# Attention and expert layers on one core: the lesser of two key tiles' negated scores is taken ahead of the exponentials, and the small constant of the softmax is added on ScalarE

## The chip, the cores and the metric

The kernel runs on one core of a Trainium2 chip, as one program. The metric is the device time of one execution in microseconds (us). The kernel before took 918.2 us (median of three runs, 917.75 to 921.53). Profiles are of one execution each.

Names used below: PE is TensorE's matmul pipe, PEld its weight load, DVE is VectorE, ACT is ScalarE, POOL is GpSimd, SP is SyncE, which issues the DMAs. SBUF is the on-chip memory, PSUM the banks that matmuls write.

## The reference, cut to what matters

Sliding-window attention (batch 4, 8 heads, 576 positions, head width 64, window 128) is followed by four experts whose outputs are mixed with given probabilities.

```python
scores = scale * np.matmul(q, k.transpose(0, 1, 3, 2))        # scale = 1/8
mask = (rel >= 0) & (rel < 128)                               # rel = query position - key position
scores = np.where(mask, scores + bias[None], -1000000000.0)   # bias = -slope * |rel|
scores = scores - np.max(scores, axis=-1, keepdims=True)
attn = np.exp(scores)
attn = attn / (np.sum(attn, axis=-1, keepdims=True) + 1e-09)
x = np.matmul(attn, v)                                        # then reshaped to 2304 tokens x 512
for e in range(4):
    h = np.maximum(x @ w1[e], 0.0)                            # 512 -> 1024
    out += p[:, e:e + 1] * (h @ w2[e])                        # 1024 -> 512
```

## The kernel before, in words

Products with float32 accuracy are made of two parts, a rounded high part and the low rest: each operand is cast to the high part (`cast`, L306, on ACT or DVE), the low part is operand minus high part (`minus`, L319, on DVE or POOL), and three matmuls (high by high, high by low, low by high) replace one. That is most of what DVE, ACT and POOL do for the experts' weights (tiles w1h, w1l, w2h, w2l) and for q, k and v (qs, kh, kl, vs).

The 2304 tokens are cut into seven blocks (`BLOCKS`, L195: three of 256, four of 384). A piece of weights is run over one or several blocks at a time. Attention for a later block is made while PE multiplies the experts of an earlier one. From about 506 us on there is no attention left and the experts of the last four blocks run in a form with seven block products instead of eight (`sevenfold`, L949).

Attention goes by units (`unit`, L487): one tile of 128 queries, two heads. A query tile sees its own 128 keys and up to 128 keys of the tile in front of it. Because the window is as wide as a tile, at each column of the two key tiles set on top of each other exactly one of the two keys is inside the window: the key in the earlier tile for columns right of the diagonal, the own one for the rest. The steps of a unit are, with their lines: scores on PE (L513); on DVE, for each head, bias added to the scores, negated and scaled, with the least value kept as the row's softmax maximum (L544, tile s of 256 columns a head, and tile t); on ACT the exponentials of each head with their sum (L556); on DVE 1e-9 added to the two sums (L571, two columns) and the reciprocal taken (L580); then the weights are multiplied by it (DVE L601 or ACT L609), transposed on PE (L627), split into high and low (L313, L323), cut into the two sides of the diagonal on POOL (L651), and multiplied with v (L698).

From block 2 on, a unit with an earlier tile is folded (`fold`, L587): the weights of the two key tiles are added to one tile of 128 columns (L592, on DVE or POOL) before they are multiplied, so that only one tile is transposed and split; L651 takes the sides apart again. There are 52 such units; 12 others (the 8 of block 1 and 4 of a tile that sees its own keys alone) are not folded, and the 8 of block 0 (`g.plain`) take a shorter way.

The order of all work is set by a planner (`Plan`, L42) in the kernel's own program: every operation is entered with the engines that it can run on, an assumed duration for each, a due time and what it reads and writes. The planner goes through time, gives each engine the operation that is due first among those that could start soon, and chooses the engine where there are two. An entry may also name a `port`: operations of DVE and POOL that name it are not planned to run at the same time (default: POOL's only). Each engine then runs its list in order, waiting on semaphores. A change of any cost or engine thus re-orders the lists of all engines, and shifts splits between DVE and POOL and casts between ACT and DVE.

Of the kernel before, what the change touches and what calls it, by code (L numbers as in the profile page):

```python
# [11 lines left out]
AF = mybir.ActivationFunctionType  # L12
ALU = mybir.AluOpType
# [3 lines left out]
NEG = -1.0e30  # L17
PE, DVE, ACT, POOL, SP = "PE", "DVE", "ACT", "POOL", "SP"
# [169 lines left out]
dve = lambda n: 0.065 + n / 960  # L188
dve2 = lambda n: 0.065 + n / 1920
pool = lambda n: 0.1 + n * 0.00256  # L190
# [12 lines left out]
FOLD = 2  # L203
# [25 lines left out]
def attention_moe(  # L229
# [13 lines left out]
    nc = tc.nc  # L243
    P = 128
# [12 lines left out]
    plan = Plan()  # L257
# [38 lines left out]
    bias = sb.tile([P, H, 2 * P], F32, tag="bias", name="bias")  # L296
# [4 lines left out]
    by = {DVE: nc.vector, POOL: nc.gpsimd}  # L301
# [38 lines left out]
    for us, nbs in passes:  # L340
        for u in us:
# [3 lines left out]
            if max(nbs) <= PAIRED and u % 2 == 0 and u + 1 in us:  # L345
                half_of[l], half_of[l + 1] = 0, 1
                for nb in nbs:
                    n = BLOCKS[nb][1]
# [14 lines left out]
            for nb in nbs:  # L363
                n = BLOCKS[nb][1]
# [25 lines left out]
    for nb, (s0, n) in enumerate(BLOCKS):  # L390
        for hp in range(NPAIR):
            g = Rec()
# [94 lines left out]
    def unit(u):  # L487
        g, pk, d = u.seg, u.pk, u.due
        n = pk + P

        o = P - pk
        edge = S - u.tile * P % S
        edge = edge if edge < P else 0
        bk, s, t = Buf("b"), Buf("acc" if g.plain else "s"), Buf("t")
        sv = lambda: s[:, : 4 * P].rearrange("p (h n) -> p h n", h=2) if s.tag == "acc" else s.place
        both = [(s, 0), (s, 1)]
# [27 lines left out]

        bkey = [("bias", g.hp)] if pk else [("bias", g.hp, 1)]
        bv = lambda: bias[:, hs, :]
        if edge:
# [7 lines left out]
            )  # L537
            bv, bkey = b2, [bb]
        if 0 < pk < P:
            plan.op({POOL: 0.3, DVE: 0.28}, lambda e: by[e].memset(sv()[:, :, :o], 0.0), d, ["scores"], both, port=())  # L540


        def least(h):
            return lambda e: nc.vector.tensor_tensor_reduce(  # L544
                out=sv()[:, h, o:],
                in0=sc()[:, h, :n],
                in1=bv()[:, h, o:],
                scale=-0.125,
                scalar=-NEG,
                op0=ALU.add,  # L550
                op1=ALU.min,
                accum_out=t[:, h : h + 1],
            )

        def exponents(h):
            return lambda e: nc.scalar.activation(  # L556
                sv()[:, h, o:],
                sv()[:, h, o:],
                AF.Exp,
                bias=t[:, h : h + 1],  # L560
                scale=-1.0,
                accum_out=t[:, 2 + h : 3 + h],
            )

        for h in range(2):
            plan.op({DVE: 0.15 + n / 960}, least(h), d + 0.3, [*bkey, bk], [(s, h), (t, h)])
        for h in range(2):
            plan.op({ACT: 0.29 + n * 0.00087}, exponents(h), d + 0.4, [(t, h)], [(s, h), (t, 2 + h)])
        plan.op(
            {DVE: 0.19},  # L570
            lambda e: nc.vector.tensor_scalar(  # L571
                out=t[:, 2:4], in0=t[:, 2:4], scalar1=1.0e-9, scalar2=None, op0=ALU.add
            ),
            d + 0.5,
            [],
            [(t, 2), (t, 3)],
# [5 lines left out]
            [(t, 2), (t, 3)],  # L582
            [(t, 4)],
        )


        fold = pk > 0 and g.nb >= FOLD  # L587
        o2, n2 = (P, P) if fold else (o, n)
        if fold:
            plan.op(  # L590
                {DVE: dve(2 * P), POOL: pool(2 * P)},
                lambda e: by[e].tensor_tensor(out=sv()[:, :, P:], in0=sv()[:, :, P:], in1=sv()[:, :, :P], op=ALU.add),  # L592
                d + 0.5,
                [(t, 2), (t, 3)],
                both,
                port=(DVE, POOL),
            )

        def weights_(e):
            if e == DVE:  # L600
# [557 lines left out]
    for hp in range(NPAIR):  # L1158
        hs = slice(2 * hp, 2 * hp + 2)
        for i, due in ((1, -37), (0, -33)):  # L1160
# [24 lines left out]
            out=dps, in0=dps, scalar1=1.0e-9, scalar2=None, op0=ALU.add  # L1185
# [9 lines left out]
            out=prob, in0=dp, in1=dps[:, :, None].to_broadcast([P, NT // P, E]), op=ALU.mult  # L1195
# [5 lines left out]
    for g in gs:  # L1201
        segment(g)
        for u in g.units:
            unit(u)
        gathered(g)
# [88 lines left out]
```

## Time and profile before

| | |
|---|---|
| runs | 917.75, 918.2, 921.53 us |
| profiled execution | 917.55 us, of which the span from first to last instruction is 915.8 us |
| PE busy | 890.8 us (97% of the span), at the full granted clock (0.999) |
| DVE busy | 735.0 us (80%), 1520 instructions |
| ACT busy | 454.3 us (50%) |
| POOL busy | 378.4 us (41%) |
| DMA | 105 GB/s mean |

Times are in us unless marked ns. A PE that is busy all the time is not losing time to waits; where its busy time falls short of a stretch, it waited, and the wait rows name what for. A mean duration of a group also holds what an instruction stood still inside.

### The profile page before, as it was taken

What the parts mean: (1) busy time and instruction counts of PE and PEld (TensorE: products, weight loads), DVE (VectorE), ACT (ScalarE), POOL (GpSimd) and SP (SyncE); (2) the same over time, 40 slices, a digit from 0 to 9 for tenths busy, and PEclk for the clock granted to TensorE, in tenths of its full rate; (3) what the DMA queues carried; (4) which work ended last, traced back from release to release, by engine and by line L of the source; (5) the groups of instructions that cost most, each with busy time, mean ns of one, the idle gap of its engine ahead of it and who ended that gap; (6) DMA issues with size and microseconds to landing.
All of it is one profiled execution on the core that took longest, in us unless ns stands there. A gap on an engine that the chain in (4) does not pass through costs nothing.

```text
span 915.8 us, 14430 instructions
## 1 busy us (share of the span) xinstructions
PE 890.8 (97%) x5108; PEld 805.5 (88%) x5108; DVE 735.0 (80%) x1520; ACT 454.3 (50%) x1089; POOL 378.4 (41%) x361
## 2 busy tenths in 40 slices
PE   7898999999999999989999999999999999999998
PEld 5787999999999998878899998989898998999897
DVE  4999887697888899989997997767876767677665
ACT  4976555364655466656664343435333433434341
POOL 2446545244444355577674663212632222222100
PEclk9999999999999999999999999999999999999999
DMA  9764534242444445443211022221232121212101
GB/s 241 234 213 160 176 123 137 81 136 67 136 135 135 131 155 178 157 127 98 82 49 67 24 90 72 68 70 52 87 116 92 47 93 47 89 50 76 40 1 70
DMA packets 39961, 96.20 MB, mean 105 GB/s; under 512 B 3792, under 2 KB 17488, under 8 KB 39888
## 3 DMA queue, kind: packets, MB, share of 16 engines
q1 hardware_dynamic: 39888, 95.28, 32.6%
q8 instruction: 40, 0.66, 0.3%
q14 instruction: 33, 0.27, 0.1%
HBM read 90.54 MB, written 4.72 MB: 104 GB/s over the span
## 4 chain that ended last, share of the span: by engine, by line
PE 84%; DVE 12%; ACT 2%; issue 1%; DMA 1%; ACTq 0%; DVEq 0%
PE b L1095 39%; PE b L907 18%; PE b L985 18%; PE av L698 3%; PE b L513 2%; PE b L627 2%; DVE w2l L323 1%; DVE s L544 1%; DVE s L592 1%; DVE w1l L323 1%; DMA k<-in_qk 1%; DVE acc L1113 1%; PE b L504 1%; DVE s L601 1%; DVE t L571 1%
## 5 line engine op out<-in xcount | busy, mean ns | idle before, releaser
L1113 DVE SCALAR_TENSOR_TENSOR acc<-b,prob,acc 128x512 f32<-128x512 f32 (+1 forms) x229 | 169.8, 743 | 66.5 <-PE b L1095 65.5
L1095 PE MATMUL b<-w2h,rh 128*128 128x512 f32 x440 | 174.1, 396 | 1.0 <-DVE rl L935 1.0
L1095 PE MATMUL b<-w2l,rh 128*128 128x512 f32 x440 | 172.9, 393 | 0.0
L1095 PE MATMUL b<-w2h,rl 128*128 128x512 f32 x440 | 172.5, 392 | 0.0
L907 PE MATMUL b<-xh,w1h 128*128 128x256 f32 (+1 forms) x528 | 160.9, 305 | 5.0 <-DVE t L544 2.1
L907 PE MATMUL b<-xl,w1h 128*128 128x256 f32 (+1 forms) x528 | 156.9, 297 | 0.5 <-DVE xl L323 0.5
L907 PE MATMUL b<-xh,w1l 128*128 128x256 f32 (+1 forms) x528 | 157.1, 297 | 0.0
L323 POOL TENSOR_TENSOR w2l<-w2r,w2h 128x512 fp32r<-128x512 f32 x45 | 67.7, 1507 | 124.9 <-ACT w2h L311 111.6
L907 PEld LDWEIGHTS b<-xh,w1h 128*128 128x128 f32 x528 | 100.2, 190 | 8.0 <-DVE t L544 2.3
L651 POOL TENSOR_SCALAR_AFFINE_SELECT pt<-s 128x512 fp32r<-128x512 f32 x104 | 66.9, 667 | 92.1 <-DVE s L323 68.5
L907 PEld LDWEIGHTS b<-xl,w1h 128*128 128x128 f32 x528 | 100.2, 190 | 2.9 <-DVE xl L323 0.7
L907 PEld LDWEIGHTS b<-xh,w1l 128*128 128x128 f32 x528 | 100.0, 189 | 0.0
L1095 PEld LDWEIGHTS b<-w2h,rl 128*128 128x128 f32 x440 | 82.6, 188 | 18.1
L1095 PEld LDWEIGHTS b<-w2h,rh 128*128 128x128 f32 x440 | 83.0, 189 | 11.9 <-DVE rl L935 1.3
L928 ACT ACTIVATE rh<-b 128x256 fp32r<-128x256 f32 (+1 forms) x132 | 53.3, 404 | 79.9 <-PE b L907 79.7
L1095 PEld LDWEIGHTS b<-w2l,rh 128*128 128x128 f32 x440 | 83.0, 189 | 10.2
L556 ACT ACTIVATE s<-s,t 128x256 f32<-128x256 f32 (+2 forms) x128 | 62.5, 489 | 59.0 <-DVE t L544 58.4
L935 DVE SCALAR_TENSOR_TENSOR rl<-b,rh 128x256 fp32r<-128x256 f32 (+1 forms) x132 | 60.1, 455 | 26.9 <-ACT rh L928 25.3
L323 POOL TENSOR_TENSOR w1l<-w1r,w1h 128x512 fp32r<-128x512 f32 x42 | 60.9, 1455 | 43.5 <-ACT w1h L311 20.7
L1019 ACT ACTIVATE xh<-b 128x384 fp32r<-128x384 f32 x46 | 22.6, 492 | 92.4 <-DVE b L1004 86.0
L311 ACT ACTIVATE w2h<-w2r 128x512 fp32r<-128x512 f32 x111 | 65.0, 621 | 6.4 <-PE b L1095 5.8
L839 POOL TENSOR_TENSOR q<-w1r 128x256 f32<-128x256 f32 x23 | 19.3, 841 | 111.3 <-DMA w1r<-in_w 85.6
(155 smaller groups left out, 2044.3 us busy)
## 6 DMA issues: line engine op xcount, KB each, us to landing
w1r<-in_w SPq DMA_DIRECT2D x60, 512.0 KB, 4.2
w2r<-in_w SPq DMA_DIRECT2D x60, 512.0 KB, 3.5
q<-in_q SPq DMA_DIRECT2D x16, 384.0 KB, 3.7
k<-in_k SPq DMA_DIRECT2D x12, 512.0 KB, 3.8
k<-in_k SPq DMA_DIRECT2D x12, 384.0 KB, 3.8
out<-acc SPq DMA_DIRECT2D x17, 256.0 KB, 2.1
v<-in_v SPq DMA_DIRECT2D x12, 256.0 KB, 2.7
v<-in_v SPq DMA_DIRECT2D x12, 192.0 KB, 3.5
```

The costliest lines, as they stand in the source:

```text
L311: nc.scalar.activation(o(), i(), AF.Copy)
L323: by[e].tensor_tensor(out=o(), in0=a(), in1=f(b()), op=ALU.subtract)
L556: return lambda e: nc.scalar.activation(sv()[:, h, o:], sv()[:, h, o:], AF.Exp, bias=t[:, h : h + 1], scale=-1.0, accum_out=t[:, 2 + h : 3 ...
L651: return lambda e: nc.gpsimd.affine_select(out=pt[:, :, :, c0 + own * P : c0 + own * P + P], in_=hl(), pattern=[[0, 4], [1, P] if own else ...
L698: nc.tensor.matmul(g.av[h][:, q0 : q0 + m], v2, g.pt[h][:, c : c + m] if g.plain else pt[:, x, h, c : c + m], start=not g.started[h], stop ...
L907: nc.tensor.matmul(bk[:, :n], a[0][:, kt, fs], b[:, kt, cols], start=kt == 0 and i == 0, stop=kt == KT - 1 and i == 2,)
L928: lambda e: nc.scalar.activation(h[:, :n], bk[:, :n], AF.Relu),
L935: lambda e: nc.vector.scalar_tensor_tensor(out=lo[:, :n], in0=bk[:, :n], scalar=0.0, in1=f(h[:, :n]), op0=ALU.max, op1=ALU.subtract,),
L985: nc.tensor.matmul(bank[:, :n], x(k), y(k), start=new and k == 0 and i == 0, stop=k == 1 and i == 2, skip_group_check=True,)
L1019: lambda e: nc.scalar.activation(h[:, :n], src(), AF.Relu),
L1095: nc.tensor.matmul(bk[:, cs], a[:, ns], b[1][:, fi, cs], start=half != 1 and fi == 0 and j == 0, stop=half != 0 and fi == 1 and j == 2, sk ...
L1113: nc.vector.scalar_tensor_tensor(out=o, in0=i_, scalar=p, in1=o, op0=ALU.mult, op1=ALU.add)
```

## The change

Three things are changed in `unit`. First, the fold is made ahead of the exponentials: the lesser of the two key tiles' negated scores is taken column by column (a masked key has a huge negated score, so the other one stays), on DVE alone, and the exponentials of a folded unit run over 128 columns a head in place of 256 or 192. The add behind the exponentials (DVE or POOL) goes. Second, the 1e-9 is added on ACT for all units but those of block 0. Third, where the earlier tile holds less than 128 keys, the unused columns are filled with a huge value and not with zero.

```diff
+        fold = pk > 0 and g.nb >= FOLD
+        o2, n2 = (P, P) if fold else (o, n)
...
-            plan.op({POOL: 0.3, DVE: 0.28}, lambda e: by[e].memset(sv()[:, :, :o], 0.0), d, ["scores"], both, port=())
+            plan.op({POOL: 0.3, DVE: 0.28}, lambda e: by[e].memset(sv()[:, :, :o], -NEG if fold else 0.0), d, ["scores"], both, port=())
...
+        def guarded(e):
+            if e == ACT:
+                nc.scalar.activation(t[:, 2:4], t[:, 2:4], AF.Copy, bias=1.0e-9)
+            else:
+                nc.vector.tensor_scalar(out=t[:, 2:4], in0=t[:, 2:4], scalar1=1.0e-9, scalar2=None, op0=ALU.add)
+
         def exponents(h):
             return lambda e: nc.scalar.activation(
-                sv()[:, h, o:],
-                sv()[:, h, o:],
+                sv()[:, h, o2:],
+                sv()[:, h, o2:],
...
+        if fold:
+            plan.op(
+                {DVE: dve(2 * P)},
+                lambda e: nc.vector.tensor_tensor(out=sv()[:, :, P:], in0=sv()[:, :, P:], in1=sv()[:, :, :P], op=ALU.min),
+                d + 0.35,
+                [(t, 0), (t, 1)],
+                both,
+                port=(DVE,),
+            )
         for h in range(2):
-            plan.op({ACT: 0.29 + n * 0.00087}, exponents(h), d + 0.4, [(t, h)], [(s, h), (t, 2 + h)])
+            plan.op({ACT: 0.29 + n2 * 0.00087}, exponents(h), d + 0.4, [(t, h)], [(s, h), (t, 2 + h)])
         plan.op(
-            {DVE: 0.19},
-            lambda e: nc.vector.tensor_scalar(
-                out=t[:, 2:4], in0=t[:, 2:4], scalar1=1.0e-9, scalar2=None, op0=ALU.add
-            ),
+            {DVE: 0.19} if g.plain else {ACT: 0.25},
+            guarded,
...
-        if fold:
-            plan.op(
-                {DVE: dve(2 * P), POOL: pool(2 * P)},
-                lambda e: by[e].tensor_tensor(out=sv()[:, :, P:], in0=sv()[:, :, P:], in1=sv()[:, :, :P], op=ALU.add),
-                d + 0.5,
-                [(t, 2), (t, 3)],
-                both,
-                port=(DVE, POOL),
-            )
```

In the new program the least-value step is L549, the 1e-9 L562 (ACT) or L564 (DVE), the exponentials L567, the new minimum L581, the reciprocal L598, the multiplication by it L606 (DVE) or L614 (ACT).

DVE's list around the last steps of one unit at about 401 to 408 us (scores of the unit in s2_77, its sums in t1_79; x0_85 and xh0_87 are another block's attention output and its high part), before:

```order
L544 ISA t1_79 128x1
L1113 SCALAR_TENSOR_TENSOR acc1_112<-b4_125,prob_132,acc1_112 128x512
L571 TENSOR_SCALAR t1_79<-t1_79 128x2
L580 RECIPROCAL t1_79<-t1_79 128x2
L540 MEMSET s1_76 128x2x64
L725 TENSOR_TENSOR x0_85<-av0_127,x0_85 64x384
L725 TENSOR_TENSOR x0_85<-av1_128,x0_85 64x384
L592 TENSOR_TENSOR s2_77<-s2_77 128x2x128
L313 CAST xh0_87<-x0_85 128x384
L601 TENSOR_TENSOR s2_77<-s2_77,t1_79 128x2x128
L323 TENSOR_TENSOR xl0_89<-x0_85,xh0_87 128x384
```

The same unit's place in DVE's list after the change:

```order
L549 ISA t1_79 128x1
L545 MEMSET s0_75 128x2x64
L730 TENSOR_TENSOR x0_85<-av0_127,x0_85 64x384
L730 TENSOR_TENSOR x0_85<-av1_128,x0_85 64x384
L549 ISA s0_75,t2_80<-b2_123,bias_130 128x192
L549 ISA t2_80 128x1
L549 ISA s0_75,t2_80<-b2_123,bias_130 128x192
L549 ISA t2_80 128x1
L313 CAST xh0_87<-x0_85 128x384
L581 TENSOR_TENSOR s2_77<-s2_77 128x2x128
L323 TENSOR_TENSOR xl0_89<-x0_85,xh0_87 128x384
```

The two-column add and the multiplication by the reciprocal are gone from DVE here; the minimum stands where the add of weights stood, but the unit's exponentials now come behind it.

ACT's list at the same unit, before:

```order
L556 ACTIVATE s2_77,t1_79<-s2_77,t1_79 128x256 x2
L722 ACTIVATE x0_85<-av0_127 64x384
L722 ACTIVATE x0_85<-av1_128 64x384
L311 ACTIVATE vs1_74<-v1_66 128x4x2x64
L311 ACTIVATE kh0_69<-k0_63 128x1024
L311 ACTIVATE qs0_67<-q0_61 128x768
```

And after:

```order
L567 ACTIVATE s2_77,t1_79<-s2_77,t1_79 128x128 x2
L311 ACTIVATE w2h0_99<-w2r0_93 128x512
L562 ACTIVATE t1_79<-t1_79 128x2
L311 ACTIVATE w2h0_99<-w2r0_93 128x512
L311 ACTIVATE kh0_69<-k0_63 128x1024
L727 ACTIVATE x1_86<-av0_127 64x384
L727 ACTIVATE x1_86<-av1_128 64x384
L614 ACTIVATE s2_77<-s2_77,t1_79 128x128 x2
```

ACT's exponentials are half as wide, the two-column add follows them behind one cast, and this unit's multiplication by the reciprocal is now ACT's.

## Rows read from the trace of the kernel before

**Rows 1.** The page's first part: busy time, share, instructions.

```profile
PE 890.8 (97%) x5108; PEld 805.5 (88%) x5108; DVE 735.0 (80%) x1520; ACT 454.3 (50%) x1089; POOL 378.4 (41%) x361
```

**Rows 2.** Busy time of each engine by stretch (us; instructions; granted clock; DMA).

```profile
core 0: us, PE busy (x) PEld busy (x) DVE busy (x) ACT busy (x) POOL busy (x), PEclk, DMA share, GB/s
...
345.00:460.00 115.00, 106.78 (x629) 96.44 (x628) 109.82 (x246) 72.30 (x187) 76.07 (x75) 1.00 0.40 128
322.00:345.00 23.00, 23.00 (x158) 21.27 (x157) 22.27 (x52) 15.29 (x43) 13.98 (x13) 1.00 0.48 155
46.00:92.00 46.00, 42.12 (x288) 38.06 (x287) 43.88 (x93) 32.60 (x84) 26.20 (x20) 1.00 0.55 184
92.00:345.00 253.00, 253.00 (x1707) 232.81 (x1706) 209.77 (x509) 136.18 (x365) 115.03 (x117) 1.00 0.40 128
```

**Rows 3.** PE's waits from 345 to 460 us: total, times, longest.

```profile
PE b L627 <- DVE s L601: 2.8, 2, 1.6
PE b L907 <- DVE t L544: 2.1, 1, 2.1
PE av L698 <- DVE x L725: 1.2, 1, 1.2
PE b L627 <- ACT s L609: 1.1, 1, 1.1
PE b L1095 <- DVE rl L935: 1.0, 1, 1.0
```

**Rows 4.** Timeline, DVE, 401 to 408 us: start, duration, instruction.

```profile
401.31 0.56 DVE L571 TENSOR_SCALAR t<-t 128x2 f32<-128x2 f32 x1
...
403.24 1.35 DVE L592 TENSOR_TENSOR s<-s 128x256 f32<-128x256 f32 x1
...
405.88 2.03 DVE L601 TENSOR_TENSOR s<-s,t 128x256 f32<-128x256 f32 x1
```

**Rows 5.** Timeline, POOL, the same stretch.

```profile
401.21 1.22 POOL L651 TENSOR_SCALAR_AFFINE_SELECT pt<-s 128x512 fp32r<-128x512 f32 x2
403.01 1.30 POOL L323 TENSOR_TENSOR vs<-v,vs 128x512 fp32r<-128x512 f32 x1 [0.58 <-ACT vs L311]
...
405.83 1.81 POOL L323 TENSOR_TENSOR qs<-q,qs 64x768 fp32r<-64x768 f32 x1
```

**Rows 6.** Timeline, PE, the wait that ends there.

```profile
407.97 0.44 PE L627 MATMUL b<-ident,s 128*128 128x128 f32 x2 [1.58 <-DVE s L601]
```

**Rows 7.** DVE's groups from 345 to 460 us: busy, mean ns, idle before.

```profile
L592 DVE TENSOR_TENSOR s<-s 128x256 f32<-128x256 f32 x13 | 10.4, 805 | 0.0
...
L323 DVE TENSOR_TENSOR w1l<-w1r,w1h 128x512 fp32r<-128x512 f32 x7 | 7.4, 1073 | 0.0
...
L571 DVE TENSOR_SCALAR t<-t 128x2 f32<-128x2 f32 x18 | 7.0, 387 | 0.6 <-ACT s L556 0.6
...
L601 DVE TENSOR_TENSOR s<-s,t 128x256 f32<-128x256 f32 x5 | 5.9, 1173 | 0.0
...
L323 DVE TENSOR_TENSOR kl<-k,kh 128x1024 fp32r<-128x1024 f32 x2 | 3.9, 1953 | 0.0
L323 DVE TENSOR_TENSOR vs<-v,vs 128x512 fp32r<-128x512 f32 x3 | 3.9, 1300 | 0.0
```

**Rows 8.** The two-column add over the whole run: ns min/median/max, first and last start.

```profile
L571 DVE TENSOR_SCALAR t<-t x72: 147/170/1804, 7.0 to 490.5; 128x2 f32<-128x2 f32 x72
```

**Rows 9.** The fold over the whole run, in the same form.

```profile
L592 DVE TENSOR_TENSOR s<-s x35: 404/416/1599, 92.2 to 478.3; 128x256 f32<-128x256 f32 x35
L592 POOL TENSOR_TENSOR s<-s x17: 732/741/1035, 97.2 to 490.6; 128x256 f32<-128x256 f32 x17
```

**Rows 10.** DVE over the whole run, two groups: busy, mean ns, idle before.

```profile
L580 DVE RECIPROCAL t<-t 128x2 f32<-128x2 f32 x72 | 11.3, 157 | 0.8
...
L323 DVE TENSOR_TENSOR qs<-q,qs 64x768 fp32r<-64x768 f32 x4 | 4.1, 1036 | 0.1
```

**Rows 11.** ACT over the whole run, the exponentials' groups.

```profile
L556 ACT ACTIVATE s<-s,t 128x256 f32<-128x256 f32 x104 | 52.2, 502 | 47.3 <-DVE t L544 46.8
...
L556 ACT ACTIVATION_READ_ACCUMULATOR s<-s,t 128x1 f32 x128 | 24.0, 188 | 0.0
...
L556 ACT ACTIVATE s<-s,t 128x192 f32<-128x192 f32 x16 | 7.2, 449 | 4.2 <-DVE t L544 4.2
...
L556 ACT ACTIVATE s<-s,t 128x128 f32<-128x128 f32 x8 | 3.2, 399 | 7.4 <-DVE t L544 7.4
```

More of the change, by code (lines that the diff above doesn't have):

```diff
@@ L584, in unit @@
         )
-        fold = pk > 0 and g.nb >= FOLD
-        o2, n2 = (P, P) if fold else (o, n)
-        if fold:
-            plan.op(
-                {DVE: dve(2 * P), POOL: pool(2 * P)},
-                lambda e: by[e].tensor_tensor(out=sv()[:, :, P:], in0=sv()[:, :, P:], in1=sv()[:, :, :P], op=ALU.add),
-                d + 0.5,
-                [(t, 2), (t, 3)],
-                both,
-                port=(DVE, POOL),
-            )
         def weights_(e):
```

## Prediction

> **What bounds the kernel now.** I read the page's busy times first: PE is busy for 890.8 us of a span of 915.8 [rows 1], so all waits of PE together are 25.0 us, and no change off PE can bring more. Next the table of busy times by stretch, to see where those 25.0 us lie. From 92 to 345 us PE is busy for 253.00 of 253 us, while attention runs beside it and DVE is busy for 209.77, that is 83% [rows 2]. Whatever gets cheaper for DVE, ACT or POOL in that stretch buys nothing. From 345 to 460 us PE is busy for 106.78 of 115, so it waits 8.2 us, and DVE is busy for 109.82, 95% [rows 2]. From 46 to 92 us PE waits 3.9 us (46 less 42.12), again with DVE at 95% (43.88) [rows 2]. The reader is to see one pattern: DVE at 83% and no wait of PE; DVE at 95% and waits. One row breaks it, and a rival rests on it: from 322 to 345 us DVE is busy for 22.27 of 23, and PE still waits for nothing [rows 2].
>
> Then PE's waits from 345 to 460 us: 2.8 us go with the multiplication by the reciprocal on DVE, 1.1 with the same on ACT, 2.1 with the least-value step, 1.2 with the sum of attention's halves and 1.0 with a rectified low part [rows 3]. These make the 8.2 us. Four of the five end with DVE.
>
> Last the timeline of one such wait, to see why DVE is late. PE starts a transpose at 407.97 us behind a wait of 1.58 us [rows 6]. DVE's multiplication started at 405.88 us and took 2.03 us; POOL ran a subtraction from 405.83 for 1.81 us, to 407.64 [rows 4, 5]. The fold at 403.24 took 1.35 us beside a POOL operation from 403.01 to 404.31, and the two-column add at 401.31 took 0.56 us beside POOL's two selects that end at 402.43 [rows 4, 5] (the first of the two ends about half way, where the add can go). So DVE stands still inside an instruction that has to wait for POOL. The two-column add shows how much: it takes 170 ns in the median and 1804 at most [rows 8], 387 ns in the mean of this stretch [rows 7], while the reciprocal, of the same two columns, takes 157 ns in the mean [rows 10].
>
> **The change part by part.** The two-column add. 64 of 72 leave DVE. In the stretch that counts these are 18, worth 7.0 us of DVE [rows 7]; without the stalls they would be 18 by 0.157, 2.8 us. So between 2.8 and 7.0 us go; the stalls may be handed to the next instruction, as weighed below. On ACT the add has no row. The nearest below is the read of an accumulator, one column, 0.188 us; the nearest above an exponential over 128 columns, 0.399 us [rows 11]. I take 0.20, next to the narrow one: 18 by 0.20 is 3.6 us, at most 7.2.
>
> The exponentials. 88 of 256 columns and 16 of 192 become 128 wide: 88 by (0.502 - 0.399) and 16 by (0.449 - 0.399) is 9.9 us less of ACT [rows 11], about a third of it from 345 to 460 us (28 and 8 of them: 3.3 us). That pays for the add. ACT is busy for 72.30 of 115 us there [rows 2], so nothing of it shows, unless an add in ACT's queue is late: in the order of the new program it stands behind one cast of weights, and the reciprocal on DVE waits for it.
>
> The fold. Before, 35 are on DVE and 17 on POOL [rows 9]; now all 52 are on DVE. Between the same two output products of PE that bound the stretch, the order has 13 on DVE before and 17 minimums now. Unstalled one takes 0.416 us [rows 9], with this stretch's stalls 0.805 [rows 7]: 7.1 to 13.7 us against 10.4 now, so -3.3 to +3.3; I take the mean with stalls less a little, +2. POOL gives up five, 0.74 us each [rows 9].
>
> What the planner moves. The multiplication by the reciprocal goes from five on DVE to one, because ACT has become the earlier engine for it: four by 1.17 us [rows 7] is 4.7 us, or 1.7 at 0.42 each without stalls; I take 3.5. Of the splits DVE loses two of kl (1.95 us each), two of vs (1.30) and two of w1l (1.07) to POOL and gets two halves of qs (1.04 us) [rows 7, 10]: 3.9 + 2.6 + 2.1 - 2.1 is 6.5 us less. POOL, busy for 76.07 us of 115 [rows 2], has room for them. The DMAs move by a place or two; PE waits for none of them in this stretch [rows 3], and PE's own work is the same.
>
> The sum for DVE from 345 to 460 us: -5 (add, between 2.8 and 7.0) +2 -3.5 -6.5 is -13 us, of 109.8: 97 us. With both ends of each, -2.8 + 3.3 - 1.7 - 6.5 is -7.7 and -7.0 - 3.3 - 4.7 - 6.5 is -21.5. Against PE's work of 106.8 us, 97 is 91% of its time, and 102 at the worst end 95%. DVE stops to be the engine that ends last for most of the stretch, but not by a wide margin. I take three quarters of the 8.2 us of waits as gone: 6.0 us. Late next is PE itself. If the cover were gone (DVE again as full as PE) the 8.2 us stay.
>
> From 46 to 92 us DVE loses six two-column adds and ACT gains them; there is no fold in that stretch. I take nothing there, and keep the 3.9 us [rows 2] as the most that it could give. Waits at the start, for the first loads, stay.
>
> So 917.55, the profiled execution's own time, less 6.0 is 911.5. The median of the runs shown is 918.2, 0.65 more; on its level the forecast is 912.2.
>
> **A rule against it.** The trace shows the fold between 404 and 1599 ns on DVE [rows 9]: it stalls beside POOL as the two-column add does. The Trainium skill (SBUF — State Buffer, "SBUF: two separate sides") says that the port pair that DVE and GpSimd share is an exclusive lock held for a whole instruction, and that a DVE operation with two SBUF inputs needs it against a GpSimd operation that reads SBUF. By that rule taking away the two-column adds hands their wait to the next instruction with two inputs, and the minimum is one. The DVE sum would then end near -8, not -13. The trace agrees as far as the rows above go.
>
> **The rivals.** First, no change that can be measured. For it: with DVE at 97% from 322 to 345 us PE waited for nothing [rows 2], so the load of DVE alone does not make waits; and 4.3 of the 8.2 us go with instructions that the change does not touch [rows 3]. The chain of a folded unit gets longer, too: the first head's exponentials now wait for the second head's least value and for the minimum (0.416 us), and gain only two by 0.10 us of width. New waits on transposes can take the place of those on the multiplication. Against it: 83% of DVE and no wait over 253 us. If only the 2.8 us on the multiplication go and half of that comes back as waits for exponentials, the time is 917.55 - 1.4, 916.2, on the median's level 916.8.
>
> Second, slower by the port. Place: DVE from 345 to 460 us. Price: before, 18 adds and 13 folds cost DVE 7.0 + 10.4 = 17.4 us [rows 7]. Seventeen minimums cost more than that from a mean of 1.02 us on. The splits that the planner hands to POOL make such a mean possible, since each keeps DVE's two-input instructions standing. At the 1.35 us that the fold took at 403.24 [rows 4] they cost 23.0 us, 5.6 more; in a stretch that DVE ends, and with the exponentials now queued behind them, that is 923.2, or 923.8 on the median's level. It decides once the mean is over 1.02 us and the other gains on DVE are eaten by stalls of the same kind. Against it: the median fold took 0.416 us [rows 9], and the planner plans no minimum beside a POOL operation, while it did plan the two-column add as if POOL did not matter.
>
> Third, more than I forecast: both stretches lose all their waits, 8.2 + 3.9 = 12.1 us, which gives 905.5, on the median's level 906.1. For it, DVE at 91% is nearer to 83% than to 95% of PE's time. Against it, from 46 to 92 us nothing is folded.
>
> **How the numbers follow.** Forecast 912.2, between 909.5 and 914.5: chance 0.50. No change, 915 to 919.5: 0.26. More than forecast, below 909.5: 0.15. Slower by the port, 920 to 926: 0.09. Half a per cent of 918.2 is 4.6 us, about what a measurement of this kernel can tell from no change: faster is below 913.6, slower above 922.8. Of the forecast 0.06 lies above 913.6, of the port rival 0.03 below 922.8. So faster 0.44 + 0.15 = 0.59; same 0.26 + 0.06 + 0.03 = 0.35; slower 0.06. The range goes from 906, the end of the third rival, to 920, where the port rival begins; about 0.13 is left out.
>
> **What would show it.** Right: in the stretch from about 345 to 460 us PE is busy for 112 us or more of 115, DVE for under 105; no wait of PE over 1 us on the multiplication by the reciprocal; the two-column add on ACT under 0.25 us; exponentials at 0.40; the minimum's mean under 0.85 us; 253 us behind 92 still full. Wrong: PE's waits there still over 6 us, under other names (transposes on exponentials, or the split behind the minimum): then order and not load made them. A minimum over 1.02 us in the mean with DVE still at 95% is the port rival. A gain from 0 to 92 us, or a loss behind 506 us where attention's end now falls later, would be something that I have not seen.

## The result, and the profile after

The changed kernel takes 909.81 us (median of four runs, 908.22 to 913.11) against 918.96 us of the kernel before in the same comparison: a ratio of 0.991, 95% interval 0.9882 to 0.9938. That is 9.15 us faster; 912.2 was forecast, and the range was 906 to 920. The profiled execution took 911.23 us, with a span of 909.5, 6.3 less than before. One profile can stand some us off its kernel's median: of 23 executions of the kernel before in the last comparison below, the five with a mean granted clock of 1.000 took 915.1 to 916.7 us, the seven with 0.996 took 921.4 to 921.9.

The table of busy times by stretch of the changed kernel (columns as in [rows 2]):

```profile
core 0: us, PE busy (x) PEld busy (x) DVE busy (x) ACT busy (x) POOL busy (x), PEclk, DMA share, GB/s
345.00:460.00 115.00, 113.72 (x673) 104.32 (x672) 100.72 (x236) 76.82 (x220) 89.44 (x82) 1.00 0.38 121
46.00:92.00 46.00, 45.84 (x322) 42.38 (x321) 39.82 (x96) 36.88 (x103) 28.17 (x22) 1.00 0.61 207
92.00:345.00 253.00, 252.66 (x1702) 232.52 (x1703) 202.99 (x489) 137.19 (x395) 112.52 (x110) 1.00 0.41 130
532.00:555.00 23.00, 20.68 (x96) 18.51 (x96) 21.27 (x30) 9.63 (x19) 12.08 (x9) 0.93 0.14 47
```

From 345 to 460 us PE waits 1.3 us where it waited 8.2 [rows 2], and DVE is busy for 100.72 us in place of 109.82, although 44 matmuls more fall into the stretch (673 against 629). From 46 to 92 us PE's waits fell from 3.9 to 0.2 us. The last row is new: from 532 to 555 us PE waits 2.3 us, at a granted clock of 0.93. The kernel before has no such place:

```profile
532.00:555.00 23.00, 23.00 (x119) 21.06 (x119) 21.61 (x37) 9.29 (x18) 14.06 (x11) 1.00 0.28 92
```

What is left of PE's waits from 345 to 460 us (five lines before [rows 3]):

```profile
PE b L632 <- ACT s L614: 0.8, 1, 0.8
PE b L1100 <- DVE rl L940: 0.4, 1, 0.4
```

DVE's groups of the same stretch that answer to [rows 7] (busy, mean ns, idle before):

```profile
L581 DVE TENSOR_TENSOR s<-s 128x256 f32<-128x256 f32 x19 | 16.7, 882 | 0.0
...
L323 DVE TENSOR_TENSOR qs<-q,qs 64x768 fp32r<-64x768 f32 x2 | 4.3, 2148 | 0.1
L323 DVE TENSOR_TENSOR w1l<-w1r,w1h 128x512 fp32r<-128x512 f32 x4 | 4.2, 1051 | 0.0
...
L606 DVE TENSOR_TENSOR s<-s,t 128x256 f32<-128x256 f32 x2 | 2.0, 1020 | 0.0
...
L323 DVE TENSOR_TENSOR vs<-v,vs 128x512 fp32r<-128x512 f32 x1 | 0.7, 679 | 0.0
```

Nineteen minimums cost 16.7 us where thirteen folds cost 10.4. The adds (7.0) are gone, the multiplications went from 5.9 to 2.0 us. Over the whole run, minimum and add (ns min/median/max), and the narrow exponentials (busy, mean ns, idle before):

```profile
L581 DVE TENSOR_TENSOR s<-s x52: 407/426/2643, 85.4 to 480.8; 128x256 f32<-128x256 f32 x52
```

```profile
L562 ACT ACTIVATE t<-t x64: 185/198/206, 35.0 to 483.3; 128x2 f32<-128x2 f32 x64
```

```profile
L567 ACT ACTIVATE s<-s,t 128x128 f32<-128x128 f32 x112 | 44.0, 394 | 42.3 <-DVE s L581 35.3 <-DVE t L549 4.0 <-DVE t L598 2.6
```

The add never stalls on ACT (206 ns at most), while on DVE it took up to 1804 [rows 8]. The minimum does stall, up to 2643 ns against a median of 426.

Where time came from and went is best read from when PE starts the same piece of work. PE runs 880 second-layer matmuls that use the rectified high part (L1095 before); the table has the start of the n-th in each trace:

| start of the n-th, us | 55th | 361st | 501st | 561st | 601st | 880th |
|---|---|---|---|---|---|---|
| before | 92.4 | 347.3 | 485.5 | 530.9 | 583.2 | 912.1 |
| changed | 89.2 | 344.3 | 474.2 | 519.9 | 576.6 | 905.8 |
| lead | 3.2 | 3.0 | 11.3 | 11.0 | 6.6 | 6.3 |

So 3 us were won before 92 us, nothing up to 347, 8.3 us by the 501st, and 4.4 us were given back at the start of the seven-product form. Of the first 3 us, 1.3 are PE's waits for the very first loads, which differ between the two executions and which the change does not touch (before, then changed):

```profile
PE b L504 <- DMA k<-in_qk: 6.1, 3, 4.4
PE b L504 <- DMA k<-in_qk: 4.8, 1, 4.8
```

At the start of the seven-product form PE waits for a DVE that is late. First PE's timeline (start, duration, instruction, idle before), then DVE's, then POOL's:

```profile
540.83 0.34 PE L990 MATMUL b<-xh,w1l 128*128 128x384 f32 x1
...
549.98 0.85 PE L990 MATMUL b<-pt,w1h 128*128 128x384 f32 x2 [1.79 <-DVE x L1067]
550.62 0.52 PE L990 MATMUL b<-pt,w1l 128*128 128x384 f32 x1
```

```profile
534.02 2.38 DVE L323 TENSOR_TENSOR w2l<-w2r,w2h 128x512 fp32r<-128x512 f32 x2
536.32 2.07 DVE L844 TENSOR_TENSOR q<-w1r 128x256 f32<-128x256 f32 x1
538.31 2.33 DVE L323 TENSOR_TENSOR w1l<-w1r,w1h 128x512 fp32r<-128x512 f32 x1
...
549.37 0.55 DVE L1067 TENSOR_TENSOR x<-b,s 128x384 f32<-128x384 f32 x1
```

```profile
535.82 4.27 POOL L844 TENSOR_TENSOR k<-k,xl 128x768 f32<-128x768 f32 x2
```

While POOL ran two element-wise operations for 4.27 us, DVE's subtraction q took 2.07 us and its w1l 2.33, where a q of the same size takes 0.42 at 542.82. The chain of work that ends in PE's matmul at 549.98 runs on DVE for all but some 2 us from 530.5 us on, these two included; DVE reached the sum that PE needed (L1067) 1.79 us late. Behind that wait a matmul of the same size takes 0.52 us in place of 0.34, and the granted clock was 0.50 (columns as in [rows 2]):

```profile
546.70:550.10 3.40, 1.61 (x8) 1.02 (x7) 3.40 (x8) 1.37 (x3) 1.53 (x2) 1.00 0.01 2
550.20:553.60 3.40, 3.40 (x12) 3.40 (x12) 2.59 (x5) 2.72 (x6) 2.52 (x2) 0.50 0.00 0
553.70:557.10 3.40, 3.40 (x20) 3.14 (x19) 3.32 (x6) 1.02 (x3) 0.49 (x1) 1.00 0.34 113
```

So the 4.4 us are 2.3 of waits, 1.7 of half speed for 3.4 us, and 0.4 that no row names.

### The profile page after: what moved, and what is told of

It is laid out like the page before. It is cut to its first block, busy times and chain, and to the rows that moved or that the text cites. A ratio compares the mean times of both kernels' runs of the same rounds, so it can differ in the third digit from the quotient of the medians.

```text
span 909.5 us, 14399 instructions
## 1 busy us (share of the span) xinstructions
PE 894.6 (98%) x5108; PEld 810.3 (89%) x5108; DVE 707.7 (78%) x1462; ACT 455.9 (50%) x1160; POOL 383.5 (42%) x353
## 4 chain that ended last, share of the span: by engine, by line
PE 92%; DVE 5%; ACT 1%; DMA 1%; POOL 1%; issue 1%; POOLq 0%; ACTq 0%
PE b L1100 41%; PE b L912 22%; PE b L990 18%; PE av L703 4%; PE b L513 3%; PE b L632 2%; PE b L504 1%; DMA k<-in_qk 1%; DVE s L581 1%; DVE acc L1118 1%; DVE w1l L323 0%; DVE w2l L323 0%; DVE q L844 0%; DVE xl L323 0%; POOL pt L656 0%
## 5 line engine op out<-in xcount | busy, mean ns | idle before, releaser
L656 POOL TENSOR_SCALAR_AFFINE_SELECT pt<-s 128x512 fp32r<-128x512 f32 x104 | 69.5, 691 | 86.5 <-DVE s L323 76.2
L323 POOL TENSOR_TENSOR w1l<-w1r,w1h 128x512 fp32r<-128x512 f32 x48 | 68.9, 1443 | 39.1 <-PE b L912 16.5
L567 ACT ACTIVATE s<-s,t 128x128 f32<-128x128 f32 (+1 forms) x128 | 52.0, 408 | 44.7 <-DVE s L581 35.3
L311 ACT ACTIVATE w2h<-w2r 128x512 fp32r<-128x512 f32 x114 | 67.5, 622 | 6.0 <-PE b L1100 5.3
L323 DVE TENSOR_TENSOR w2l<-w2r,w2h 128x512 fp32r<-128x512 f32 x72 | 62.4, 880 | 1.2 <-ACT w2h L311 0.9
```

The source lines that it names most:

```text
L311: nc.scalar.activation(o(), i(), AF.Copy)
L323: by[e].tensor_tensor(out=o(), in0=a(), in1=f(b()), op=ALU.subtract)
L567: return lambda e: nc.scalar.activation(sv()[:, h, o2:], sv()[:, h, o2:], AF.Exp, bias=t[:, h : h + 1], scale=-1.0, accum_out=t[:, 2 + h : ...
L656: return lambda e: nc.gpsimd.affine_select(out=pt[:, :, :, c0 + own * P : c0 + own * P + P], in_=hl(), pattern=[[0, 4], [1, P] if own else ...
```

## The experiments

The load theory: the two-column add's stalls on DVE made DVE late, and taking the add away is the gain. Its rivals: a new order of the lists is the gain; the stall only moves on; the minimum is the gain. Each run has its own kernel before on the same chip (medians 917.1 to 917.2).

**The add on ACT, all lists kept (f1_eps).** All engines' lists are those of the kernel before; only the add is issued elsewhere.

```diff
+        def guarded(e):
+            if not g.plain:
+                nc.scalar.activation(t[:, 2:4], t[:, 2:4], AF.Copy, bias=1.0e-9)
...
-            lambda e: nc.vector.tensor_scalar(
-                out=t[:, 2:4], in0=t[:, 2:4], scalar1=1.0e-9, scalar2=None, op0=ALU.add
-            ),
+            guarded,
```

> The kernel before with every engine's list kept as it was; only the two-column add of the 64 units behind block 0 is issued on ACT, at the same place of the program. Load theory (DVE's stalls on the add made PE's waits): from 345 to 460 us DVE loses 3 to 7 of 109.8 us, PE's 8.2 us of waits there fall to about 5, and the run is 3 to 4 us faster than the kernel before (about 915). Order theory (the new lists made the gain): within 1.5 us of the kernel before. Hand-over theory (the stall goes to DVE's next instruction): DVE's mean fold or multiplication rises by 0.2 us or more and the time stays.

914.19 us, ratio 0.9966 (0.9945 to 0.9986): 3.0 us faster. The stretch from 345 to 460 us:

```profile
345.00:460.00 115.00, 108.44 (x638) 98.47 (x638) 106.07 (x233) 75.24 (x211) 77.99 (x79) 1.00 0.41 129
```

PE waits 6.6 us, not 8.2. DVE lost 3.7 us there, though the adds took 7.0. Over the run DVE's busy time fell by 22.7 us (735.0 to 712.3), but that does not measure what is handed on: neighbouring instructions overlap a little in the trace, and busy time counts the overlap once. With durations added up instead, 31.6 us of adds left DVE and all its other instructions, the same ones in the same order, grew by 4.8 us: about a seventh of the adds' time is handed on, or a fifth of what they stood still (31.6 less 64 by 0.157 us). The fold's mean over the run went from 631 to 674 ns and the multiplication's of the same shape from 740 to 650, so the 0.2 us of the hand-over theory are not there. The load theory fits, but the waits in the stretch fell less than it said, and of 5.3 us of lead in this profile 3.0 came before 92 us.

**Both parts in the old lists, flawed (f2_min, f3_both).** The minimum is issued behind the second least-value step, the exponentials of folded units run over 128 columns, the fold behind them goes, lists otherwise kept; f3 has the add on ACT as well.

```diff
         def least(h):
+            def emit(e):
+                least_(h)
+                if fold and h == 1:
+                    nc.vector.tensor_tensor(out=sv()[:, :, P:], in0=sv()[:, :, P:], in1=sv()[:, :, :P], op=ALU.min)
...
-                lambda e: by[e].tensor_tensor(out=sv()[:, :, P:], in0=sv()[:, :, P:], in1=sv()[:, :, :P], op=ALU.add),
+                lambda e: None,
```

> The kernel before with every list kept; the minimum is issued on DVE right behind the second least-value step of a folded unit, the add of weights behind the exponentials goes (35 on DVE, 17 on POOL), the exponentials of folded units run over 128 columns. Load theory: DVE gets 17 more of about 0.42 to 0.8 us, five of them from 345 to 460 us (2 to 4 us), ACT loses 9.9 us that nobody waits for: 0 to 4 us slower than the kernel before. Order theory: within 1.5 us. If the fold's place behind the exponentials was what made the multiplication late: 2 to 3 us faster.

> Both of the above in the lists of the kernel before: all instructions of the changed kernel, but no list planned anew apart from the minimum's place. Load theory: most of the change's 9 us is there without new lists, 3 us faster than before at least. Order theory: within 2 us of the kernel before, and the whole 9 us come from the planner.

930.57 us, 1.0143 (1.0109 to 1.0177), and 921.52 us, 1.0028 (1.0009 to 1.0048). In the old lists the first head's exponentials can stand ahead of the second head's least value. In such units these kernels take the minimum over exponentials and not over scores, and DVE waits for ACT at 16 of the minimums of f3. So they answer another question than was asked, and I draw nothing from them.

**The same, mended (f3_both2).** Both heads' exponentials are issued at the place of the second.

```diff
-            return lambda e: nc.scalar.activation(
...
+            def emit(e):
+                for x in ((), (0, 1))[h] if fold else (h,):
+                    nc.scalar.activation(
...
```

> Both parts of the change in the lists of the kernel before, as in the run before it, with its flaw mended: both heads' exponentials of a folded unit are now issued together, at the place of the second, so that none stands ahead of the minimum. Load theory: the eps part alone was worth 3 us in these lists; with 17 more minimums on DVE (about 0.5 to 0.8 us each, 8 to 13 us, hidden for the most part) 0 to 4 us faster than the kernel before. If the minimum ahead of the exponentials needs lists planned for it: 0 to 5 us slower than before, with PE's waits on transposes and on attention's sums.

920.25 us, 1.0034 (1.0018 to 1.005): 3.1 us slower than before, and 6.1 us slower than the add alone in the same lists. The longest of PE's waits from 345 to 460 us, 8.4 us in all:

```profile
PE b L1112 <- DVE rl L952: 3.0, 2, 1.7
PE av L715 <- DVE x L742: 2.1, 1, 2.1
PE b L644 <- ACT s L626: 1.7, 1, 1.7
```

Two of the three are on DVE and one on ACT, and the change touches none of these operations. That they come late because DVE now has 52 folds in place of 35 is likely and not shown. The minimum's part of the change costs, in lists that are not made for it.

**The changed kernel with the add back on DVE, lists kept (g1_epsback).**

```diff
-            if e == ACT:
+            if False:
```

> The changed kernel with its lists kept; only the two-column add is issued on DVE again, at the same place of the program, where it can stall beside POOL. Load theory: 64 adds of 0.17 to 0.5 us come back, 18 of them from 345 to 460 us (3 to 8 us, DVE from 100.7 to over 105): 2 to 5 us slower than the changed kernel, 912 to 915. Order theory: within 1 us of the changed kernel's 909.8.

913.63 us, 0.9955 (0.9936 to 0.9974), against 0.991 (0.9882 to 0.9938) of the changed kernel: about 4 us back, as the load theory has it, though the two intervals just touch and the two profiled executions are 1.6 us apart. The add stalls again (ns min/median/max):

```profile
L564 DVE TENSOR_SCALAR t<-t x72: 148/170/2375, 7.1 to 486.4; 128x2 f32<-128x2 f32 x72
```

The place is not the one expected: DVE is busy for 102.8 us from 345 to 460 us, not for over 105. The lead at the 475th product is that of the changed kernel (12.9 against 12.7 us); from there to the 501st this run loses 4.2 us and the changed kernel 1.4.

**Each part with new lists (r1_eps, r2_min), and a new order alone (c1_nudge).**

The first is the kernel before with the add planned and issued on ACT (`guarded` as in f1_eps), the second the changed kernel with the add planned and issued on DVE, the third the kernel before with one number of the planner moved.

```diff
-            {DVE: 0.19},
-            lambda e: nc.vector.tensor_scalar(
-                out=t[:, 2:4], in0=t[:, 2:4], scalar1=1.0e-9, scalar2=None, op0=ALU.add
-            ),
+            {DVE: 0.19} if g.plain else {ACT: 0.25},
+            guarded,
```

```diff
-            {DVE: 0.19} if g.plain else {ACT: 0.25},
+            {DVE: 0.19},
```

```diff
-EXTRA = 0.03
+EXTRA = 0.031
```

> The two-column add on ACT alone, the fold left as a sum behind the exponentials, and all lists planned anew for it. Load theory: 64 stalls less on DVE as in the run with the old lists (3 us), and the planner can use the room: 3 to 6 us faster than before. If the minimum is what the new lists need: 1 to 3 us faster.

> The minimum ahead of the exponentials alone, the two-column add left on DVE, all lists planned anew. Load theory: DVE keeps its 33 us of two-column adds and gets 17 folds more, the planner hands splits to POOL: 0 to 4 us faster than before. If the two parts only work together: not faster than before.

> The kernel before with one number of the planner moved from 0.030 to 0.031, so that all lists are planned anew with the same instructions: what a new order is worth by itself. Load theory: within 3 us of the kernel before, PE's waits from 345 to 460 us over 5 us. If a new order by itself explains the change: 5 us or more away from the kernel before, on either side.

The add alone: 905.83 us, 0.9881 (0.9862 to 0.9901). The minimum alone: 914.5 us, 0.9971 (0.9959 to 0.9983). The nudge: 920.63 us, 1.003 (1.0009 to 1.0051), 3.5 us slower, between the 3 and the 5 of its two expectations; PE's waits in its stretch from 345 to 460 us were 3.2 us, where over 5 were expected. So the add on ACT, with lists planned for it, gives all of the change's gain: 11.3 us, over the 3 to 6 that I expected; with the old lists it gave 3.0. The minimum alone is 2.6 us faster than before, less than the nudge moves. In the fastest kernel PE waits for one thing from 345 to 460 us:

```profile
PE b L631 <- ACT s L613: 0.9, 1, 0.9
```

```profile
345.00:460.00 115.00, 114.08 (x676) 104.48 (x675) 100.78 (x243) 79.81 (x226) 84.31 (x90) 1.00 0.38 121
506.00:916.00 410.00, 393.32 (x1968) 354.06 (x1966) 291.51 (x458) 148.80 (x287) 111.90 (x97) 1.00 0.20 65
```

From 506 us to the span's end at 902.8 PE is idle for 3.5 us. The kernel before is idle for 3.3 from there to its end at 915.8, so nothing is given back at the seven-product form:

```profile
506.00:916.00 410.00, 406.50 (x2035) 366.33 (x2033) 302.15 (x473) 154.84 (x296) 119.07 (x100) 1.00 0.20 66
```

**Is it a lucky order? (r1_nudge, after_nudge).** The number EXTRA moved from 0.03 to 0.031, the edit just shown, in the add-alone kernel and in the changed one.

> The add on ACT alone with new lists, as in the fastest run so far (0.988 of before), with the planner's one number moved from 0.030 to 0.031: another order of the same instructions. If the gain is the add's: still 7 us or more faster than before (0.992 or less). If it was a lucky order: within 4 us of before.

> The changed kernel with the same number moved. If the minimum costs some 2 to 5 us beside the add on ACT: 0.989 to 0.995 of before, and slower than the run beside it. If the difference between the two was order alone: it can as well come out faster than that run.

907.14 us, 0.9888 (0.9858 to 0.9918), and 912.35 us, 0.9938 (0.9919 to 0.9958). In two orders each, the add alone is 10 to 11 us faster than before, the add with the minimum 5 to 9, the kernel before and its nudge 3.5 us apart. An order alone moved these kernels by 1 to 4 us, the add with new lists by more than that. The minimum costs 2.7 us by the ratios of the first pair, whose intervals overlap, and 5.2 us in the second, where they do not. Two orders are few for the size.

Where the parts act is seen best between two of PE's products, the 361st and the 561st, since a stretch of fixed times holds other work in each run. All attention is done by the 561st:

| run | add on | minimum | lists | 361st to 561st, us | PE's waits | DVE busy |
|---|---|---|---|---|---|---|
| before | DVE | no | its own | 183.6 | 8.2 | 91% |
| c1_nudge | DVE | no | new | 182.3 | 4.2 | 89% |
| f1_eps | ACT | no | as before | 181.3 | 6.6 | 88% |
| r1_eps | ACT | no | new | 175.5 | 1.0 | 88% |
| r1_nudge | ACT | no | new | 174.7 | 0.9 | 89% |
| f3_both2 | ACT | yes | as before | 187.2 | 9.6 | 88% |
| r2_min | DVE | yes | new | 178.9 | 2.8 | 90% |
| g1_epsback | DVE | yes | as changed | 178.5 | 3.1 | 89% |
| changed | ACT | yes | its own | 175.6 | 1.3 | 87% |
| after_nudge | ACT | yes | new | 176.1 | 1.5 | 87% |
| p1_port (below) | DVE | no | new | 183.5 | 7.4 | 85% |
| j2_ahead (below) | ACT | yes | new | 177.8 | 2.9 | 88% |

The times of c1_nudge, f3_both2 and p1_port each hold 3.4 us at half clock, some 1.7 us of them lost. Three things follow. With lists kept, the add is worth 2.3 us here (before and f1_eps) and 2.9 (g1_epsback and changed); the other 5.8 us of r1_eps came with the lists that the planner made for it, and one new order with the add on DVE (c1_nudge) gave 1.3, or some 3 without its half clock. Whether the planner used the room or met good orders, two orders cannot say. Next, beside the add in new lists the minimum costs little here (175.6 and 176.1 against 175.5 and 174.7). From the 561st to the 601st product, at the start of the seven-product form, the two kernels with it lose 4.4 and 5.1 us against before, and the two without it nothing: that is the main part of its price. Last, DVE's busy share does not order PE's waits: they are 7.4 us at 85%, 1.0 and 6.6 at 88%, and 2.8 at 90%.

**Was it the plan's ignorance? (p1_port).** The kernel before, with the add planned as an operation that POOL excludes.

```diff
             [(t, 2), (t, 3)],
+            port=(DVE,),
         )
```

> The kernel before, computing the same on the same engines, but the planner is told that the two-column add on DVE stands still while POOL works (it is planned like the other two-port operations). If the gain came from plans that the hidden stall had made wrong: 3 us or more faster than before. If it came from taking the work off DVE: within 3 us of before, on either side.

922.15 us, 1.0047 (1.0028 to 1.0067): 4.9 us slower, which neither expectation had. The add still took 490 ns in the mean over its 72 instructions; in the kernel before it took 460 (this run, then before):

```profile
L571 DVE TENSOR_SCALAR t<-t 128x2 f32<-128x2 f32 x72 | 35.2, 490 | 3.4 <-ACT s L556 2.3 <-ACT acc L556 0.7
L571 DVE TENSOR_SCALAR t<-t 128x2 f32<-128x2 f32 x72 | 33.2, 460 | 9.4 <-ACT s L556 8.2 <-ACT acc L556 0.7
```

Telling the planner did not take the stall away. Taking the work off DVE did.

**The start of the seven-product form (j2_ahead).** The changed kernel with another AHEAD.

```diff
-AHEAD = 30.0
+AHEAD = 36.0
```

> The changed kernel with attention planned to end 36 us and not 30 us ahead of the seven-product form. Its profile lost 4.7 us of its lead between 512 and 577 us: PE waited 2.3 us there, and the granted clock stood at half for 3.4 us behind the longer wait. If the shorter way from attention's end to that form is the cause: no wait of PE over 1 us and no half clock there, 2 to 4 us faster than the changed kernel (0.987 to 0.989 of before). If the wait is DVE's and POOL's queue whatever the distance: the same as the changed kernel, 0.991.

909.14 us, 0.9904 (0.9873 to 0.9934): as a time, not told apart from the changed kernel, where 0.987 to 0.989 was expected if the distance is the cause. In its profile (span 905.4) the wait there is short, and no stretch behind it is at half clock:

```profile
PE b L990 <- DVE x L1067: 0.7, 2, 0.4
```

Against it the nudged change has 3.2 us in the same place:

```profile
PE b L990 <- DVE x L1067: 3.2, 1, 3.2
```

From the start of attention's last product to the first seven-product matmul it is 31.4 us before and 27.6 after, and 28.7 in this run, so the edit moved it by 1.1 us only. Of twelve traces (all but f2_min and f3_both) the five with 30.1 us or more lose nothing there (the 561st to the 601st product take 52.3 us; the changed kernel needs 56.7); the seven with less lose 0.7 to 5.1 us. In these traces the loss came only with a short way, but the way does not size it: the minimum alone has 25.2 us and loses 0.7. What sets the size stays open.

## Why the prediction was right, point by point

- **The bound** held. The stretch from 92 to 345 us gave nothing (lead 3.2 us at its start, 3.0 at its end), and the gain came where DVE was at 95%.
- **From DVE's load to PE's waits** is the weak step. The forecast let three quarters of the waits go because DVE's sum would fall to 91% of PE's time. The waits did go, but in the table of twelve runs 88% of DVE goes with 1.0 us of waits and with 6.6, and the lowest share, 85%, with 7.4. So the lists, that is which instruction stands late, counted at least as much as DVE's load; why the good lists are good is not shown.
- **The add.** Taken as 2.8 to 7.0 us less for DVE in the stretch, and 0.20 us on ACT: 0.198 measured. Alone, with lists kept, it brought DVE 3.7 us and the run 3.0. Of 31.6 us of adds, 4.8 came back in DVE's other instructions, about a seventh. The Trainium skill (SBUF — State Buffer, "SBUF: two separate sides") says that the port pair of VectorE and GpSimd is an exclusive lock, held for a whole instruction. The hand-over that the prediction drew from it is there for that seventh only, and it does not cancel the gain.
- **The fold** was the term that was set wrong: I priced it at +2 us of DVE beside a gain on ACT that nobody waits for, so nearly neutral. Beside the add on ACT it costs the run 6.1 us in the old lists and 2.7 and 5.2 us in new ones, and in new ones mainly at the start of the seven-product form, where I had no term. The minimum's mean in the stretch was 0.882 us, over the 0.85 that I named, and under the 1.02 of the port rival. The stalls of that rival are there (2643 ns at most); what part of the price they are is not shown.
- **What the planner moves.** Multiplications 3.5 us less were forecast, 3.9 measured. The two halves of qs on DVE took 3.02 and 1.27 us, not 1.04 each; the longer ran beside a POOL subtraction. DVE fell by 9.1 us in the stretch, where I had 13 (between 7.7 and 21.5), with more work of PE served.

```profile
421.37 3.02 DVE L323 TENSOR_TENSOR qs<-q,qs 64x768 fp32r<-64x768 f32 x1
421.00 2.57 POOL L323 TENSOR_TENSOR kl<-k,kh 128x1024 fp32r<-128x1024 f32 x1
```

- **The sum.** In the profiled execution 6.0 us were forecast and 6.3 measured. That closeness is luck, two offsets that cancel: 8.3 us won from 347 us to the 501st product instead of 6.0, 3 us won before 92 us where I took nothing, and 4.4 us lost at the start of the seven-product form, which I named only as something that I had not seen. By the medians 9.15 us were won.
- **The no-change rival** claimed that order and not load makes the waits. The time that it gave, 916.8, did not come: a new order with the same instructions moved the kernel before by 3.5 us, to the slower side, and with the add on ACT two orders kept the gain. It was right that load alone does not make waits, and most of the gain of the add came only with new lists (11.3 us against 3.0).

The version to keep is the add on ACT with the fold left behind the exponentials: 905.83 us, faster than the kernel before in both orders, and than the changed kernel clear of noise in one pair of the two.

## What to carry to other kernels

Here a two-column VectorE instruction took up to ten times its median beside GpSimd work: look at the minimum, median and maximum of each group, not at its mean, and try the tiny one on another engine. When a change has two parts, time them apart: here one part paid for the other. Where a planner orders the work, time each part with the lists kept and with new lists, and a nudge of the kernel before as well; its spread is what a new order alone is worth. And compare runs between the same two products, not between the same two times.

## What the runs showed of the hardware that I had not expected

All 29 of the two-column adds over 300 ns in the kernel before end within 31 ns of the end of a POOL instruction, so the long ones stood until POOL was done. Planning the add as excluded by POOL left its mean at 490 ns; its longest there was 2322 ns.

After some waits of PE the granted clock was at 0.50, the lower of its two levels (1.2 and 2.4 GHz), for 3.4 us (6.8 once): behind the wait of 1.79 us at 548 us in the changed kernel, and behind one of 1.01 us at 85 us in r2_min. Other waits were followed by none: the one of 2.10 us at 361 us in the kernel before, and in g1_epsback one of 1.79 us again, for the same sum, behind which the matmuls kept their speed:

```profile
552.55 0.62 PE L990 MATMUL b<-pt,w1h 128*128 128x384 f32 x2 [1.79 <-DVE x L1067]
553.00 0.34 PE L990 MATMUL b<-pt,w1l 128*128 128x384 f32 x1
```

So the 1.7 us of half speed in the changed kernel's profile are not a sure part of its time.
